# Splitting weights while attention runs: the second halves' word added by VectorE, split sums in the weighted values' bank

## The chip, the cores and the metric

One Trainium2 chip, one core. The metric is the device time of one execution in microseconds. The engines are TensorE (PE for matmuls, PEld for its weight loads), VectorE (DVE), ScalarE (ACT), GpSimd (POOL) and the DMA queues (SPq is issued by SyncE, ACTq by ScalarE). PSUM is what TensorE writes and VectorE and ScalarE read.

## The reference

Attention over 8 batches, 8 heads, 576 positions and 64 channels, where each row keeps its 32 largest scores; the result, as 4608 tokens of 512 channels, goes through a gated feed-forward layer (512 to 1536 to 512). The feed-forward weights are float64, everything else float32.

```python
scores = scale * np.matmul(q, k.transpose(0, 1, 3, 2))
kth = np.partition(scores, -top_k, axis=-1)[..., -top_k:-top_k + 1]
scores = np.where(scores >= kth, scores, -1000000000.0)
attn = np.exp(scores - np.max(scores, axis=-1, keepdims=True))
attn = attn / (np.sum(attn, axis=-1, keepdims=True) + 1e-09)
x = np.matmul(attn, v)        # then to tokens x channels
gate = 1.0 / (1.0 + np.exp(-(x @ w_gate)))
out = (gate * (x @ w_val)) @ w_out
```

## The kernel before

**Attention steps.** `run` (L603) goes through 160 steps: 8 batches, 4 pairs of heads, 5 tiles of rows. In step n TensorE computes the scores of step n + 2 (`begin`, L285 to L328), VectorE and GpSimd choose the 32 largest of step n (`select`), and TensorE transposes the numerators of step n - 2 (`turn`, L425). When a block of tiles is done, `weigh` (L463) multiplies them by the values into one PSUM tile `po` of pool `ps_o`, which has one buffer, and `scale` (L496) lets VectorE divide by the sums (`xf`, L485) and ScalarE and GpSimd split the result into two float32r parts, `xh` and `xl`.

**Feed-forward.** `ffn` (L514) works on 256 tokens at first and on 384 later. Each product is made of three float32r matmuls (L540 to L542 into `pz`, L564 to L566 into `po2`, shown as `po`), with weights in two parts. `pz` and `po2` are in pool `ps_f`, with three buffers. `more` runs as many of these matmuls between the pieces of a step as a table (`PACE`) allows.

**Splitting the weights.** Each of the 18 weight tiles [128, 2, 512] of float64 arrives as pairs of 32-bit words and is split half by half, 36 halves in all. `split_front` (L179) makes `bits`, a float32 from the upper word (ScalarE L190, VectorE L191, L192), `power`, its exponent in bfloat16 (VectorE L193, one buffer), `frac`, the lower word as a number (ScalarE L195) times `power` (GpSimd L197, two pieces), and `pair[:, 0]`, the upper part of the word rounded to float32r (ScalarE L198). `split_back` (L201) forms the rest on TensorE in a PSUM tile `rest` of pool `ps_f`: `ident` times `bits` (L205, a float32 matmul, which the trace shows as two instructions), minus `pair[:, 0]` (L206), plus 2**-52 times `frac` (L207). ScalarE copies `rest` into `pair[:, 1]` (L209), and the ScalarE queue issues the DMA that stores the pair in DRAM for later units (L210). `bits` has three buffers.

**When the halves are split.** The first 8 halves (`2 * LOADED`) go one by one through steps 0 to 7, before any feed-forward work. The other 28 are split while the first unit of 256 tokens goes through the feed-forward layer: at each piece of a step at most one `split_back`, once its front is more than three pieces old, and then the next `split_front`, as long as fewer than three halves wait. `load` inside `ffn` also calls both, where a weight is needed that is not ready.

**What sets the order.** TensorE's instructions run in the order of the program, written by hand (`manual_schedule`). The order of each other engine's instructions is set by a planner that runs the program against a model of time; `urgent()` gives an instruction precedence there. A buffer of a pool is written again only when its last reader is done, so pools make engines wait for each other.

Of the kernel before, what the change touches and what calls it, by code (L numbers as in the profile page):

```python
# [10 lines left out]
F32 = mybir.dt.float32  # L11
# [3 lines left out]
F32R = mybir.dt.float32r  # L15
BF16 = mybir.dt.bfloat16
FP8 = mybir.dt.float8e4
AF = mybir.ActivationFunctionType
ALU = mybir.AluOpType
# [11 lines left out]
def tile_topk_attention_then_gated_ffn(  # L31
# [8 lines left out]
    nc = tc.nc  # L40
    P = 128
    B, H, _, S = k.shape
# [10 lines left out]
    M = NP * P  # L53
# [27 lines left out]
    LOADED = 4  # L81
# [8 lines left out]
    bi = ctx.enter_context(tc.tile_pool(name="bi", bufs=4))  # L90
    b2 = ctx.enter_context(tc.tile_pool(name="b2", bufs=2))
    bk = ctx.enter_context(tc.tile_pool(name="bk", bufs=2 * NP))
    bv = ctx.enter_context(tc.tile_pool(name="bv", bufs=3))
    bs = ctx.enter_context(tc.tile_pool(name="bs", bufs=4))
    bq = ctx.enter_context(tc.tile_pool(name="bq", bufs=3))
    bqr = ctx.enter_context(tc.tile_pool(name="bqr", bufs=4))
    bkr = ctx.enter_context(tc.tile_pool(name="bkr", bufs=2))
# [6 lines left out]
    ps_o = ctx.enter_context(tc.tile_pool(name="ps_o", bufs=1, space=bass.MemoryType.PSUM))  # L104
    ps_f = ctx.enter_context(tc.tile_pool(name="ps_f", bufs=3, space=bass.MemoryType.PSUM))

    ident = const.tile([P, P], F32, tag="ident", name="ident")
# [26 lines left out]
    def behind_scores():  # L134
        return tc.issue_after(evicted[-1].ins) if len(evicted) < 12 else ExitStack()

    def urgent():
        return tc.high_priority() if stated else ExitStack()
# [10 lines left out]
    stored, splits, waiting, fetched, ticks, evicted, due, later, pinned, raw_loads = set(), {}, [], {}, [0], [], [], [], [], []  # L149

    pre = ExitStack()
    pre_pools = {n: pre.enter_context(tc.tile_pool(name=n, bufs=bufs)) for n, bufs in (("signs", 1), ("raw", 3), ("parts", 3), ("power", 1))}
    plus, minus = [pre_pools["signs"].tile([P, P], F32R, tag=t, name=t) for t in ("plus", "minus")]
    nc.scalar.activation(plus, ident, AF.Copy, scale=2.0**-52)
    nc.scalar.activation(minus, ident, AF.Copy, scale=-1.0)

    split_order = order[KEPT:LOADED] + order[:KEPT] + order[LOADED:]
    halves_of_weights = [(t, i) for t in split_order for i in range(2)]
# [9 lines left out]
    def load_raw(idx, i):  # L168
        raws[idx, i] = raw = pre_pools["raw"].tile([P, NP * P, 2], U32, tag="raw", name=f"wraw_{idx}_{i}")
        ins = load(raw.rearrange("p n t -> p (n t)"), w[idx][:, i * NP * P : (i + 1) * NP * P].bitcast(U32))  # L170
        raw_loads.append(ins.ins)

    def split_front(idx, i):

        if i == 0:
            splits[idx] = pools["w"].tile([P, 2, 2, NP, P], F32R, tag="w", name=f"wsplit_{idx}")
        at = halves_of_weights.index((idx, i))
        for ahead in halves_of_weights[at : at + 2]:
            if ahead not in raws:  # L179
                load_raw(*ahead)  # L180
        raw = raws[idx, i]
        low, top = raw[:, :, 0], raw[:, :, 1]
        pair = splits[idx][:, i].rearrange("p a c n -> p a (c n)")
        bits = pre_pools["parts"].tile([P, NP * P], F32, tag="bits", name=f"wbits_{idx}_{i}")
        frac = pair[:, 1]
        word = bits.bitcast(U32)
        power = pre_pools["power"].tile([P, NP * P], BF16, tag="power", name=f"wpower_{idx}_{i}")
        heads = bits.bitcast(U16).rearrange("p (n t) -> p n t", t=2)[:, :, 1]
        with behind_scores():
            nc.scalar.activation(bits, top.bitcast(F32), AF.Copy, scale=2.0**-112)  # L190
        nc.vector.tensor_scalar(word, word, 3, None, op0=ALU.logical_shift_left)  # L191
        nc.vector.scalar_tensor_tensor(word, top, 0x80000000, word, op0=ALU.bitwise_and, op1=ALU.bitwise_or)  # L192
        nc.vector.tensor_scalar(power.bitcast(U16), heads, 0xFF80, None, op0=ALU.bitwise_and)  # L193
        with behind_scores():
            nc.scalar.activation(frac, low, AF.Copy)  # L195
        for c in (slice(0, 2 * P), slice(2 * P, 4 * P)):
            nc.gpsimd.tensor_tensor(frac[:, c], frac[:, c].bitcast(F32), power[:, c], op=ALU.mult)  # L197
        nc.scalar.activation(pair[:, 0], bits, AF.Copy)  # L198
        waiting.append((idx, i, pair, bits, ticks[0]))

    def split_back():  # L201
        idx, i, pair, bits, _ = waiting.pop(0)
        frac = pair[:, 1]
        rest = ps_f.tile([P, M], F32, tag="f", name=f"wrest_{idx}_{i}")
        nc.tensor.matmul(rest, ident, bits, start=True, stop=False)  # L205
        nc.tensor.matmul(rest, minus, pair[:, 0], start=False, stop=False)  # L206
        nc.tensor.matmul(rest, plus, frac, start=False, stop=True)  # L207
        with urgent():
            nc.scalar.activation(pair[:, 1], rest, AF.Copy)  # L209
        nc.scalar.dma_start(w_split[idx][:, i], pair.bitcast(F32))  # L210
        if i == 1:
            stored.add(idx)
# [23 lines left out]
    def next_front():  # L236
        while len(waiting) > 2:
            split_back()
        split_front(*due.pop(0))
# [94 lines left out]
    def masked(J, s, kth, st, e, nm, place=None):  # L334

        for j in range(J):
            nc.vector.scalar_tensor_tensor(  # L337
                e[:, j], s[:, j], kth[j], e[:, j], op0=ALU.is_ge, op1=ALU.mult, accum_out=st[:, 4 + j : 5 + j]
            )
        nc.vector.tensor_scalar(st[:, 4 : 4 + J], st[:, 4 : 4 + J], 1e-9, None, op0=ALU.add)  # L340
        if place is not None:
            x, k, rows = place
            invs = inverses[x]
            sums = st[:, 4:6] if J == 2 else st[:, 4:5].to_broadcast([P, 2])
            nc.vector.reciprocal(invs[:, k:8:4], sums)
            if k == 3:
                turned_invs = b6[0].tile([P, 32], F32, tag="invt", name=f"invt_{nm}")
                nc.vector.transpose(turned_invs, invs)
                for x in range(4):
                    nc.sync.dma_start(rows[:, 32 * x : 32 * x + 32], turned_invs[32 * x : 32 * x + 8])  # L350
            return e, None
        nc.vector.reciprocal(st[:, 6 : 6 + J], st[:, 4 : 4 + J])
        inv = bi.tile([P, P], F32, tag="inv", name=f"inv_{nm}")
        nc.gpsimd.tensor_copy(
            inv.rearrange("p (j d) -> p j d", j=J), st[:, 6 : 6 + J].unsqueeze(2).to_broadcast([P, J, P // J])
        )
        return e, inv
# [19 lines left out]
    def select(J, s, col, nm, place):  # L377
# [42 lines left out]
        for j in range(J):  # L420
            nc.vector.max(kths[:, at[j] : at[j] + 8], u[:, j])  # L421
        yield masked(J, s, [kths[:, a + 7 : a + 8] for a in at], st, e, nm, place)

    def turn(e, inv, i, et, nm):
# [85 lines left out]
    def ffn(nm0, xs, t0, width, early, last):  # L510
# [7 lines left out]
        def load(idx):  # L518
            if not (t0 == 0 and early):
                return stored_weight(idx, nm0)  # L520
            first_weights(order.index(idx))
            while idx not in stored:
                if not waiting:
                    next_front()
                split_back()
            return fetched[idx]
# [72 lines left out]
    def run(general):  # L599
# [160 lines left out]
        for n in range(len(steps) + 3):  # L760
# [6 lines left out]
            if splitting:  # L767
                split_front(*fronts.pop(0))
# [24 lines left out]
            else:  # L793
# [9 lines left out]
                for t, chunk in enumerate(chunks):  # L803
                    ticks[0] += 1
                    if not fronts and not splitting:
                        if waiting and ticks[0] - waiting[0][4] > 3:
                            split_back()
                        if due and len(waiting) < 3:
                            next_front()
                    if chunk is not None:  # L810
                        next(chunk, None)
                        while unfinished and t == 0:
                            weighted(*unfinished.pop(0))
                    elif 3 <= n:
                        weighed(n - 3)
                        if n == OPEN:
                            weighed(n - 2)
                    if t == 2 and splitting and len(waiting) > 1:
                        split_back()
                    if n != OPEN or t > 0:  # L820
                        more(begun + (goal - begun) * (t + 1) / len(chunks))
# [84 lines left out]
```

## Time and profile before

| | |
|---|---|
| median of 3 runs | 1576.34 us (1575.83 to 1578.79) |
| profiled execution, its own time | 1575.44 us |
| its span, first to last instruction | 1573.6 us |
| TensorE busy | 1500.9 us (95%) |
| VectorE busy | 1289.7 us (82%) |
| ScalarE busy | 1151.0 us (73%) |
| GpSimd busy | 1106.5 us (70%) |
| granted TensorE clock, mean | 0.988 of 2.4 GHz |

The page gives the share of busy time of each engine over the whole span. Since the kernel has stages with different limits, the tables by stretch, the waits and the chain have to be read beside it. Ends of matmuls are modelled; what one matmul really takes is read from the distance between the starts of two that follow each other.

### The profile page before, as it was taken

To read this page: it belongs to the slowest core of one execution; us is meant where nothing else is said; L and a number is where in the kernel's file an instruction comes from. 1 tells how busy PE (TensorE), PEld (TensorE's weight loads), DVE (VectorE), ACT (ScalarE), POOL (GpSimd) and SP (SyncE) were. 2 spreads that over 40 slices of the span, in tenths; PEclk is the share of its full clock that TensorE was granted. 3 is DMA by queue.
4 is the path that set the end of the run, shared out by engine and by line. 5 is a ranking of instruction groups with operands and counts; after the bars stand their busy time and mean duration, and the time that the engine had idled before them with its cause. 6 is when DMAs were issued, how large, how long until landed. Compare 5 with 4: busy or idle time off the path is not lost.

```text
span 1573.6 us, 33616 instructions
## 1 busy us (share of the span) xinstructions
PE 1500.9 (95%) x10242; PEld 1310.9 (83%) x10242; DVE 1289.7 (82%) x5996; ACT 1151.0 (73%) x2520; POOL 1106.5 (70%) x1656
## 2 busy tenths in 40 slices
PE   5777999999999999999999999999999999999998
PEld 2355768988898899888898899888898899889897
DVE  7988878899999788999888788999888788998001
ACT  6868987888687678777777778777777778777321
POOL 4657897698776876887775876887775876775312
PEclk9889999999999999999999999999999999999999
DMA  6426878778665676676565675676555666564575
GB/s 204 151 93 221 274 274 303 270 250 299 228 214 190 228 260 204 212 254 211 198 210 190 228 257 206 213 251 213 199 209 190 228 224 224 198 217 168 208 271 186
DMA packets 96240, 347.34 MB, mean 221 GB/s; under 512 B 13105, under 2 KB 33585, under 8 KB 68273
## 3 DMA queue, kind: packets, MB, share of 16 engines
q1 hardware_dynamic: 90864, 326.22, 60.4%
q10 hardware_dynamic: 5184, 18.88, 3.0%
q8 instruction: 83, 1.36, 0.4%
q14 instruction: 109, 0.88, 0.2%
HBM read 316.60 MB, written 28.45 MB: 219 GB/s over the span
## 4 chain that ended last, share of the span: by engine, by line
PE 63%; DVE 11%; POOL 4%; ACT 4%; issue 2%; DMA 2%; ACTq 0%; SPq 0%; DVEq 0%; POOLq 0%
PE pz L540 10%; PE pz L542 9%; PE pz L541 9%; PE pss L316 7%; PE po L480 7%; PE pt L432 5%; PE po L564 5%; PE po L566 5%; PE po L565 5%; DVE e L337 3%; DVE cand L394 3%; POOL u L413 2%; DVE kths L421 2%; DVE cand L400 1%; ACT under L407 1%
## 5 line engine op out<-in xcount | busy, mean ns | idle before, releaser
L413 POOL TENSOR_TENSOR u<-s,under 128x288 f32<-128x288 f32 x576 | 423.9, 760 | 128.8 <-ACT under L407 124.1
L540 PE MATMUL pz<-xh,w 128*128 128x384 f32 (+1 forms) x1152 | 404.3, 351 | 0.0
L394 DVE MAX8 cand<-s 128x8 f32<-128x72 f32 x2304 | 352.9, 217 | 38.1 <-ACT s L324 26.5
L542 PE MATMUL pz<-xh,w 128*128 128x384 f32 (+1 forms) x1152 | 377.4, 328 | 0.0
L541 PE MATMUL pz<-xl,w 128*128 128x384 f32 (+1 forms) x1152 | 376.9, 327 | 0.0
L407 ACT ACTIVATE under<-s,leads 128x576 fp8e4<-128x576 f32 x288 | 222.6, 773 | 103.8 <-DVE leads L398 97.0
L337 DVE SCALAR_TENSOR_TENSOR e<-s,kths,e 128x576 f32<-128x576 f32 x288 | 282.9, 990 | 15.0 <-ACT e L332 14.4
L421 DVE MAX8 kths<-u 128x8 f32<-128x584 f32 x288 | 219.3, 761 | 66.1 <-POOL u L414 63.6
L552 POOL TENSOR_TENSOR gl<-gf,gh 128x384 fp32r<-128x384 f32 (+1 forms) x156 | 156.3, 1002 | 121.1 <-ACT gh L551 118.1
L540 PEld LDWEIGHTS pz<-xh,w 128*128 128x128 f32 x1152 | 217.1, 188 | 5.7 <-DVE tops L398 1.3
L332 ACT ACTIVATE e<-s,st 128x576 f32<-128x576 f32 x288 | 208.9, 771 | 15.7 <-PE pt L432 10.7
L541 PEld LDWEIGHTS pz<-xl,w 128*128 128x128 f32 x1152 | 217.7, 189 | 0.8
L542 PEld LDWEIGHTS pz<-xh,w 128*128 128x128 f32 x1152 | 216.5, 188 | 0.0
L438 ACT ACTIVATE ring<-pt 128x384 f32<-128x384 f32 x336 | 163.5, 496 | 56.9 <-PE pt L432 56.0
L432 PE MATMUL pt<-ident,e 128*128 128x128 f32 x1152 | 191.9, 276 | 7.8 <-ACT ring L438 7.8
L432 PEld LDWEIGHTS pt<-ident,e 128*128 128x128 f32 x1152 | 147.2, 141 | 39.4 <-ACT ring L438 11.2
L564 PE MATMUL po<-w,gh 128*128 128x512 f32 x408 | 173.1, 424 | 1.2 <-DVE gf L550 1.2
L324 ACT ACTIVATE s<-pss 128x576 f32<-128x576 f32 x256 | 164.2, 641 | 8.8 <-PE pss L316 8.3
L316 PE MATMUL pss<-k,qh 128*128 128x288 f32 (+2 forms) x588 | 162.2, 294 | 8.2 <-ACT s L324 7.9
L550 DVE SCALAR_TENSOR_TENSOR gf<-gf,pz 128x384 f32<-128x384 f32 (+1 forms) x156 | 79.7, 511 | 102.6 <-PE pz L542 90.4
L565 PE MATMUL po<-w,gl 128*128 128x512 f32 x408 | 160.9, 394 | 2.8 <-POOL gl L552 2.8
L566 PE MATMUL po<-w,gh 128*128 128x512 f32 x408 | 161.3, 395 | 0.0
(115 smaller groups left out, 3315.8 us busy)
## 6 DMA issues: line engine op xcount, KB each, us to landing
w<-ws SPq DMA_DIRECT2D x216, 1024.0 KB
v<-in_v_dram SPq DMA_DIRECT2D x68, 320.0 KB
wraw<-in_w_dram SPq DMA_DIRECT2D x36, 512.0 KB
ws<-wsplit ACTq DMA_DIRECT2D x36, 512.0 KB
qraw<-in_q_dram SPq DMA_DIRECT2D x140, 128.0 KB
kraw<-in_k_dram SPq DMA_DIRECT2D x56, 288.0 KB
out_dram<-acc SPq DMA_DIRECT2D x36, 256.0 KB
invb<-rows SPq DMA_DIRECT2D x66, 128.0 KB
```

Source lines behind the costliest of these rows:

```text
L316: nc.tensor.matmul(ps[:, half, o : o + n], x[:K, h * P : (h + 1) * P], ks[h][:K, k0 : k0 + n], start=t == 0, stop=t == len(todo) - 1,)
L337: nc.vector.scalar_tensor_tensor(e[:, j], s[:, j], kth[j], e[:, j], op0=ALU.is_ge, op1=ALU.mult, accum_out=st[:, 4 + j : 5 + j])
L394: nc.vector.max(cand[:, j, 8 * g : 8 * g + 8], s[:, j, g * SEG : (g + 1) * SEG])
L413: nc.gpsimd.tensor_tensor(u[:, j, c], s[:, j, c], under[:, j, c], op=ALU.mult)
L421: nc.vector.max(kths[:, at[j] : at[j] + 8], u[:, j])
L432: nc.tensor.transpose(pt[:, c], ef[:, k0 : k0 + P], ident)
L540: nc.tensor.matmul(ps[:, R], wt[:, u, 0, d], xh[:, R], start=d == 0, stop=False)
L541: nc.tensor.matmul(ps[:, R], wt[:, u, 0, d], xl[:, R], start=False, stop=False)
L542: nc.tensor.matmul(ps[:, R], wt[:, u, 1, d], xh[:, R], start=False, stop=d == NP - 1)
L564: nc.tensor.matmul(outs[r], gh, wh, start=f == 0, stop=False)
L565: nc.tensor.matmul(outs[r], gl, wh, start=False, stop=False)
L566: nc.tensor.matmul(outs[r], gh, wl, start=False, stop=f == FG - 1)
```

## The change

- In `split_back`, second halves (`i == 1`) that are not among the first 8 get no `ident` times `bits` matmul. The accumulation begins with minus `pair[:, 0]`, and VectorE adds `bits` when it reads `rest`, in place of ScalarE's copy. All other halves keep matmul and copy.
- `rest` is taken from pool `ps_o` (one buffer, shared with `po` of the weighted values), no longer from `ps_f`.
- `frac` is scaled by -2**-52 when ScalarE makes it, so that `minus` serves for both matmuls; `plus` and the instruction that makes it are gone.
- `power` has two buffers. `inv` moves from a pool with four buffers to one of its own with three.

```diff
+    binv = ctx.enter_context(tc.tile_pool(name="binv", bufs=3))
...
-    pre_pools = {n: ... for n, bufs in (("signs", 1), ("raw", 3), ("parts", 3), ("power", 1))}
-    plus, minus = [pre_pools["signs"].tile([P, P], F32R, tag=t, name=t) for t in ("plus", "minus")]
-    nc.scalar.activation(plus, ident, AF.Copy, scale=2.0**-52)
+    pre_pools = {n: ... for n, bufs in (("signs", 1), ("raw", 3), ("parts", 3), ("power", 2))}
+    minus = pre_pools["signs"].tile([P, P], F32R, tag="minus", name="minus")
     nc.scalar.activation(minus, ident, AF.Copy, scale=-1.0)
...
-            nc.scalar.activation(frac, low, AF.Copy)
+            nc.scalar.activation(frac, low, AF.Copy, scale=-(2.0**-52))
...
-        rest = ps_f.tile([P, M], F32, tag="f", name=f"wrest_{idx}_{i}")
-        nc.tensor.matmul(rest, ident, bits, start=True, stop=False)
-        nc.tensor.matmul(rest, minus, pair[:, 0], start=False, stop=False)
-        nc.tensor.matmul(rest, plus, frac, start=False, stop=True)
+        rest = ps_o.tile([P, M], F32, tag="o", name=f"wrest_{idx}_{i}")
+        added = i == 1 and (idx, i) not in halves_of_weights[: 2 * LOADED]
+        if not added:
+            nc.tensor.matmul(rest, ident, bits, start=True, stop=False)
+        nc.tensor.matmul(rest, minus, pair[:, 0], start=added, stop=False)
+        nc.tensor.matmul(rest, minus, frac, start=False, stop=True)
         with urgent():
-            nc.scalar.activation(pair[:, 1], rest, AF.Copy)
+            if added:
+                nc.vector.tensor_tensor(pair[:, 1], rest, bits, op=ALU.add)
+            else:
+                nc.scalar.activation(pair[:, 1], rest, AF.Copy)
         nc.scalar.dma_start(w_split[idx][:, i], pair.bitcast(F32))
...
-        inv = bi.tile([P, P], F32, tag="inv", name=f"inv_{nm}")
+        inv = binv.tile([P, P], F32, tag="inv", name=f"inv_{nm}")
```

## Rows read from the trace of the kernel before

**Rows 1.** The page: busy time by engine, and the chain that ended last.

```profile
PE 1500.9 (95%) x10242; PEld 1310.9 (83%) x10242; DVE 1289.7 (82%) x5996; ACT 1151.0 (73%) x2520; POOL 1106.5 (70%) x1656
...
PE 63%; DVE 11%; POOL 4%; ACT 4%; issue 2%; DMA 2%; ACTq 0%; SPq 0%; DVEq 0%; POOLq 0%
```

**Rows 2.** Windows: stretch, length, busy us by engine, clock, DMA share, GB/s.

```profile
118.00:157.00 39.00, 31.05 (x164) 20.18 (x162) 34.47 (x128) 33.58 (x70) 30.76 (x45) 1.00 0.66 223
157.00:197.00 40.00, 38.41 (x219) 28.45 (x217) 35.84 (x117) 36.22 (x75) 32.60 (x43) 1.00 0.81 272
197.00:245.00 48.00, 44.07 (x234) 30.92 (x233) 36.70 (x112) 40.63 (x84) 43.98 (x63) 1.00 0.81 274
...
245.00:1560.00 1315.00, 1301.35 (x9229) 1180.97 (x9226) 1077.93 (x5141) 956.04 (x2125) 932.52 (x1390) 1.00 0.65 225
```

**Rows 3.** The chain that ended last, 196 to 245 us, shares by line.

```profile
by line: DMA kraw<-in_k_dram 24.4%; ACT wsplit L195 7.0%; issue 6.8%; ACT wbits L190 4.7%; DVE wbits L192 4.4%; ACT k L265 3.9%; POOL k L267 3.6%; DVE e L337 3.4%; ACT wsplit L198 3.4%; DVE wbits L191 3.3%; PE po L480 3.3%; ACT wsplit L209 
```

**Rows 4.** One tile, wrest, 118 to 245 us: duration ns min/median/max, starts, forms.

```profile
L205 PE MATMUL wrest<-wbits,ident x56: 590/592/697, 120.1 to 241.1; 128*128 128x512 f32 x56
...
L209 ACT ACTIVATE wsplit<-wrest x28: 572/592/653, 125.7 to 243.5; 128x512 fp32r<-128x512 f32 x28
```

**Rows 5.** Timeline of TensorE: start us, us, instruction; one half of the 28.

```profile
229.14 1.02 PE L205 MATMUL wrest<-wbits,ident 128*128 128x512 f32 x2
229.60 0.79 PE L206 MATMUL wrest<-wsplit,minus 128*128 128x512 f32 x1
230.23 0.39 PE L207 MATMUL wrest<-wsplit,plus 128*128 128x512 f32 x1
230.46 0.29 PE L316 MATMUL pss<-k,qh 128*128 128x288 f32 x1
```

**Rows 6.** TensorE's waits, 118 to 245 us: us in total, times, longest.

```profile
PE wrest L205 <- DVE gf L550: 6.4, 5, 2.4
PE pz L540 <- ACT wsplit L209: 3.7, 3, 2.1
...
PE wrest L205 <- ACT wsplit L209: 1.4, 2, 1.0
```

**Rows 7.** Timeline, TensorE and ScalarE: longest and shortest wait for the copy.

```profile
130.16 0.39 PE L207 MATMUL wrest<-wsplit,plus 128*128 128x512 f32 x1
...
136.72 0.57 ACT L209 ACTIVATE wsplit<-wrest 128x512 fp32r<-128x512 f32 x1
...
188.47 0.40 PE L207 MATMUL wrest<-wsplit,plus 128*128 128x512 f32 x1
...
189.02 0.59 ACT L209 ACTIVATE wsplit<-wrest 128x512 fp32r<-128x512 f32 x1
...
189.75 1.04 PE L205 MATMUL wrest<-wbits,ident 128*128 128x512 f32 x2
```

**Rows 8.** Timeline around 210 us: weighted values right behind a first half.

```profile
210.04 0.43 PE L480 MATMUL po<-ring,v 128*64 128x256 f32 x1
...
213.77 0.60 ACT L209 ACTIVATE wsplit<-wrest 128x512 fp32r<-128x512 f32 x1
```

**Rows 9.** VectorE by line and form, whole span: busy us, mean ns, idle before.

```profile
L550 DVE SCALAR_TENSOR_TENSOR gf<-gf,pz 128x384 f32<-128x384 f32 x120 | 65.1, 543 | 96.6 <-PE pz L542 87.0 <-ACT gf L547 9.2
...
L575 DVE SCALAR_TENSOR_TENSOR acc<-po,acc 128x512 f32<-128x512 f32 x3 | 2.1, 692 | 6.2 <-PE po L566 5.5 <-DMA out_dram<-acc 0.7
```

**Rows 10.** Waits of VectorE, then of ScalarE, 118 to 245 us.

```profile
DVE wpower L193 <- POOL wsplit L197: 8.2, 9, 2.4
DVE wbits L191 <- ACT wbits L190: 5.7, 3, 2.5
...
ACT wsplit L198 <- DVE wbits L192: 5.3, 4, 2.4
```

**Rows 11.** Windows, a later stretch of 20 us.

```profile
340.00:360.00 20.00, 19.14 (x137) 18.19 (x138) 19.23 (x101) 16.70 (x38) 17.68 (x26) 0.91 0.85 267
```

**Rows 12.** Timeline of TensorE: the stand at 340 us.

```profile
340.86 0.56 PE L565 MATMUL po<-w,gl 128*128 128x512 f32 x1 [2.78 <-POOL gl L552]
```

More of the change, by code (lines that the diff above doesn't have):

```diff
@@ L151, in tile_topk_attention_then_gated_ffn @@
     pre = ExitStack()
-    pre_pools = {n: pre.enter_context(tc.tile_pool(name=n, bufs=bufs)) for n, bufs in (("signs", 1), ("raw", 3), ("parts", 3), ("power", 1))}
-    plus, minus = [pre_pools["signs"].tile([P, P], F32R, tag=t, name=t) for t in ("plus", "minus")]
-    nc.scalar.activation(plus, ident, AF.Copy, scale=2.0**-52)
+    pre_pools = {n: pre.enter_context(tc.tile_pool(name=n, bufs=bufs)) for n, bufs in (("signs", 1), ("raw", 3), ("parts", 3), ("power", 2))}
+    minus = pre_pools["signs"].tile([P, P], F32R, tag="minus", name="minus")
     nc.scalar.activation(minus, ident, AF.Copy, scale=-1.0)
```

## The prediction

> **What bounds the kernel now.** The page comes first: TensorE is busy for 95% of the span, the next engine, VectorE, for 82%, and 63% of the chain that ended last lies on TensorE [rows 1]. So the kernel as a whole is bound by TensorE, and whatever is won before a stretch in which TensorE never stands is won at the end. The windows say where that holds [rows 2]. From 245 us on, when the last weight is split, TensorE is busy for 1301 of 1315 us. From 118 to 245 us, where the 28 halves are split that the change touches, four engines are nearly full: summed over the three windows of 127 us, TensorE 113.5, ScalarE 110.4, VectorE 107.0, GpSimd 107.3 us. Then I read the chain for the end of this stage [rows 3]: between 196 and 245 us it runs over key loads (24.4%) and over splitting and attention work of ScalarE, VectorE and GpSimd; TensorE appears there only with `po` (3.3%), behind the last half. So in the splitting stage TensorE's work is not simply the bound, and TensorE, whose order is fixed, often stands for a buffer.
>
> **TensorE's work.** Of the 28 halves (L209 28 times, L205 56 times, two for each [rows 4]), 14 are second halves. What L205 really takes is read from starts [rows 5]: a half lasts 230.46 - 229.14 = 1.32 us; L207 takes 230.46 - 230.23 = 0.23, and L206 has the same shape and type, so 1.32 - 2 x 0.23 = 0.86 us are L205's. 14 x 0.86 = 12.0 us of TensorE's work go.
>
> **TensorE's stands for `ps_f`.** L205 waited 6.4 us for VectorE's `gf` and 1.4 us for ScalarE's L209; both are waits for one of three `ps_f` buffers, and go, since `rest` no longer lies there. `pz` waited 3.7 us for L209 [rows 6]. The smallest of the three, 0.4 us, is `pz` waiting for its own weights, and stays; 3.3 go. Together 6.4 + 1.4 + 3.3 = 11.1 us.
>
> **New stands for `ps_o`.** There is one buffer now for `rest` and `po`, so the matmuls of a half wait until the half before has been read, and `po` waits for the half before it. TensorE runs in order: behind such a wait stand feed-forward, transposes and scores. The trace of before has no such wait, so I bound it. From the end of L207 to the end of L209 a first half took between 0.74 us (189.61 - 188.87) and 6.74 us (137.29 - 130.55) [rows 7], in the mean of the 14 first halves 3.0 us; the following second half came about 1.0 us after L207's end (0.88 in rows 7), stands taken off. If all copies came as fast as the fastest one, 13 pairs would cost nothing; if all stay as late as they were, the differences pair by pair add up to 25.0 us. At four places `po` or its reader stands right beside a half. The clearest is at 210.04 us, where `po` begins while the copy of the first half in front of it ends at 214.37 [rows 8]. With the shortest latencies these places cost 2.9 us in all, with the recorded ones 12.2. So the new stands lie between 2.9 and 37.2 us. I take a latency of 1.8 us, midway between fastest and mean: ScalarE loses 14 copies of 0.592 us, 8.3 of its 110.4 busy us [rows 2, 4], and works off its queue whenever TensorE stands. 13 x (1.8 - 1.0) = 10.4, and 6 for the four places: 16.4 us.
>
> TensorE's balance: 12.0 + 11.1 - 16.4 = 6.7 us won.
>
> **VectorE.** It gets 14 additions of 128x512 from PSUM and SBUF into float32r. The nearest row is the last accumulation, L575, same shape and one operand in PSUM: 692 ns; 128x384 took 543 ns [rows 9], which is the low end. 14 x 0.692 = 9.7 us. The second buffer of `power` ends its waits of 8.2 us for GpSimd [rows 10]: L193 no longer stands for the half before. What is late next is L191 for ScalarE (5.7 us), which has less to do than before. VectorE's position changes by 9.7 - 8.2 = +1.5 us (between -8.2 and +9.7 if only one holds). It has 20 us without work in these 127, and I count 1.5 us against the gain.
>
> **ScalarE.** The copies save 8.3 us. Against that its queue now holds 14 DMA issues (L210 of before) that wait for VectorE's addition instead of ScalarE's own copy, and behind each stand its next activations. The nearest row is ScalarE's wait for VectorE at L198: 5.3 us over 26 instructions, 4 of them waiting [rows 10], 0.2 us each, so 14 x 0.2 = 2.8 us; bounds 0 and 14 x 2.4 = 34 us, the longest wait every time. ScalarE stays ahead by about 5.5 us, which covers this. [...]
>
> **Costed at nothing.** The scale in L195 is a field of an instruction that runs anyway. `plus` was made in the opening, before there is anything to split. `bits` of a second half is held until the addition, up to some 2 us longer; a front of three halves later needs it, and halves come 4.5 us apart (127 / 28). `inv` with three buffers: written in one step and read in the next, so two are alive. The first 8 halves now share `ps_o` with `po` too, but before the feed-forward work begins, when TensorE has least to do; if that cover is gone, four meetings at the shortest latency cost 3 us. The planner will order the later stages anew: it may lose or repeat a stand like the 2.78 us at 340.86 [rows 12], a few us of either sign, and I take 0.
>
> **Sum.** -6.7 + 1.5 = -5.2 us. The profiled execution took 1575.4 us, 0.9 less than the median; 1575.4 - 5.2 = 1570.2, and on the median's footing 1571.
>
> **Rivals.**
> 1. *The three others decide, no change.* For it: TensorE's 3.3% of the chain in [rows 3], and VectorE at 107 + 9.7 = 117 of 127 us. Against it: TensorE is 96% busy from 157 to 197 us [rows 2]. Then only VectorE's +1.5 us and a part of ScalarE's gain count: between -2 and +5 us, 1574 to 1581, in the middle 1577.
> 2. *The one bank stops TensorE, slower.* Place: each second half behind its first half, and `po` behind a half. For it: the mean latency was 3.0 us, and the gain is used up from 2.3 us on ((12.0 + 11.1 - 6) / 13 + 1.0 = 2.3). Against it: ScalarE was late partly because it stood itself for VectorE [rows 10], whose longest cause goes. Price with latencies as recorded: 25.0 + 12.2 - 23.1 = +14 us, 1590; most likely half of it, 1583. A long stand can also lower the clock: behind the stand of 2.78 us [rows 12] the mean granted clock of 20 us was 0.91 [rows 11], so a part ran at 1.2 GHz, which costs 0.09 x 20 = 1.8 us each time, while the 2.4 us stand of [rows 6] left 1.00 [rows 2]. [...]
> 3. *The copies follow at once, much faster.* For it: latencies of 0.74 us occur. 12.0 + 11.1 - 2.9 = 20 us at most; ScalarE and VectorE, at 84 to 87% of the stage, will not let all of it through: -10 to -18 us, in the middle 1562.
> 4. *It does not do what it says:* excluded, the matmuls are left out in the program, and TensorE's order is the program's.
>
> **From cases to numbers.** My forecast (-2 to -10 us, 1566 to 1574) has 0.45, of which 0.07 lie within 0.2% (3.2 us, what a measurement here can tell from no change). Rival 1 has 0.20 (0.14 within, 0.06 slower), rival 2 has 0.18, rival 3 has 0.17. Faster 0.38 + 0.17 = 0.55, same 0.21, slower 0.24. The range reaches from -15 to +6 us and leaves out about 0.05 of rival 3 and 0.11 of rival 2: 1561 to 1582.
>
> **What will show it.** 28 matmul instructions of L205 fewer, all in second halves; the 14 additions near 0.69 us; no wait of L193 for L197; no wait of TensorE's `rest` for `gf`. TensorE's waits for L209, the addition and `xf` at `rest` and `po` should sum to about 16 us; above 23 the forecast is wrong in that term. The stage that ended at 245 us should end about 5 us earlier, and the rest of the span should shift with it; if the stage ends earlier but the end does not, a later stage took it back.

## Result: slower, and where the time went

The changed kernel takes 1589.0 us (1588.9 to 1589.5, 4 runs) against 1576.4 before; the ratio is 1.0082 (95% interval 1.0068 to 1.0095). 1571 was forecast, with 1561 to 1582 as the range: the wrong side, and outside. The page of the changed kernel, engines and chain, answers to [rows 1]:

```profile
PE 1497.7 (94%) x10214; PEld 1312.5 (83%) x10214; DVE 1295.8 (82%) x6010; ACT 1144.9 (72%) x2505; POOL 1100.5 (69%) x1656
...
PE 66%; DVE 11%; ACT 6%; POOL 4%; issue 2%; DMA 2%; SPq 0%; ACTq 0%; DVEq 0%; POOLq 0%
```

28 TensorE instructions are gone, but its busy time fell by 3 us, not by 12. To see why, I compare the stage over the same work in every kernel: from the 73rd feed-forward matmul to the 180th transpose. Windows of the kernel before, and of the changed kernel (columns as in [rows 2]):

```profile
119.40:255.10 135.70, 122.22 (x681) 87.03 (x681) 112.53 (x370) 116.02 (x239) 113.76 (x159) 1.00 0.77 262
```

```profile
122.50:268.80 146.30, 118.99 (x654) 88.77 (x653) 118.99 (x382) 110.20 (x225) 108.99 (x159) 0.92 0.73 243
```

The stage begins 3.1 us late and lasts 10.6 us longer; it ends 13.7 us late. The span is 14.1 us longer, so the 1319 us behind the stage cost nothing worth naming. The 10.6 us have three parts. TensorE stood for 135.7 - 122.2 = 13.5 us before and for 146.3 - 119.0 = 27.3 after: +13.8. The granted clock was 1.00 and is 0.92: by my estimate up to 0.08 x 146.3 = 11.7 us of the busy time are there only because a part of it ran at half clock. Windows of 1 us of the changed kernel give 0.50 from 220 to 222 us, and matmuls of 512 columns start 0.43 us apart there (219.75, 220.18, 220.60, 221.03); at 1.00 they start 0.23 us apart (254.83, 255.06, 255.28, 255.51). The 1.2 and 2.4 GHz of the recorded texts are these clocks of 0.50 and 1.00: 512 columns in 0.427 us are 1.2 per ns, which by estimate makes 2.4 at 1.00, where 0.23 us show 2.2. What is left, the work at full clock, is 119.0 - 11.7 = 107.3 instead of 122.2: -14.9. 13.8 + 11.7 - 14.9 = 10.6. (The clock is given to 0.01, so the last two are good to 0.7 us, and TensorE also stood in a little of the time at half clock, 1.7 of the 3 us from 185 to 188, so both are rather too large than too small.) Work was saved as forecast, a little more even; stands and the lower clock took it back and more.

TensorE's waits in the changed kernel from 118 to 262 us, which answer to [rows 6], with L207 the identity matmul, L208 and L209 the two with `minus`, L214 ScalarE's copy, L212 VectorE's addition:

```profile
PE wrest L208 <- ACT wsplit L214: 21.6, 9, 3.8
PE po L485 <- DVE wsplit L212: 2.0, 2, 1.0
PE wrest L208 <- DVE xf L490: 1.6, 1, 1.6
PE wrest L207 <- DVE xf L490: 1.1, 1, 1.1
PE po L485 <- ACT wsplit L214: 0.9, 1, 0.9
```

Each of the five is a wait for the one buffer of `ps_o`, and they sum to 27.2 us. The waits for `ps_f` of [rows 6] are gone. The longest, in the timeline of ScalarE and TensorE:

```profile
217.23 0.57 ACT L214 ACTIVATE wsplit<-wrest 128x512 fp32r<-128x512 f32 x1
...
217.86 0.50 PE L208 MATMUL wrest<-wsplit,minus 128*128 128x512 f32 x1 [3.80 <-ACT wsplit L214]
218.19 0.39 PE L209 MATMUL wrest<-wsplit,minus 128*128 128x512 f32 x1
```

The second half's first matmul starts 0.06 us after the copy of its first half ends, and no other TensorE work comes in between: windows of 1 us from 215 to 217 us show it busy for 0.00 us. Nine of 14 second halves stand like this.

VectorE and ScalarE in the changed kernel: the addition, the DMA issue's wait in ScalarE's queue (duration ns min/median/max), and two of VectorE's waits, which answer to [rows 10]:

```profile
L212 DVE TENSOR_TENSOR wsplit<-wrest,wbits x14: 667/676/692, 133.0 to 256.4; 128x512 fp32r<-128x512 f32 x14
...
L215 ACTq EVENT_SEMAPHORE  x16: 17/17/2304, 125.7 to 255.1; - x16
```

```profile
DVE wbits L191 <- ACT wbits L190: 10.7, 10, 2.3
...
DVE wpower L193 <- POOL wsplit L197: 0.5, 1, 0.5
```

### The profile page after: what moved, and what is told of

Its sections match the earlier page's. It is cut to its first block, busy times and chain, and to the rows that moved or that the text cites. A ratio compares the mean times of both kernels' runs of the same rounds, so it can differ in the third digit from the quotient of the medians.

```text
span 1587.7 us, 33557 instructions
## 1 busy us (share of the span) xinstructions
PE 1497.7 (94%) x10214; PEld 1312.5 (83%) x10214; DVE 1295.8 (82%) x6010; ACT 1144.9 (72%) x2505; POOL 1100.5 (69%) x1656
## 4 chain that ended last, share of the span: by engine, by line
PE 66%; DVE 11%; ACT 6%; POOL 4%; issue 2%; DMA 2%; SPq 0%; ACTq 0%; DVEq 0%; POOLq 0%
PE pz L545 10%; PE pz L547 9%; PE pz L546 9%; PE pss L321 8%; PE po L485 7%; PE pt L437 6%; PE po L569 5%; PE po L570 5%; PE po L571 5%; DVE cand L399 3%; DVE e L342 3%; DVE kths L426 2%; POOL u L418 2%; DMA kraw<-in_k_dram 1%; ACT under L412 1%
## 5 line engine op out<-in xcount | busy, mean ns | idle before, releaser
L412 ACT ACTIVATE under<-s,leads 128x576 fp8e4<-128x576 f32 x288 | 222.6, 773 | 107.3 <-DVE leads L403 97.7
L557 POOL TENSOR_TENSOR gl<-gf,gh 128x384 fp32r<-128x384 f32 (+1 forms) x156 | 156.7, 1005 | 124.7 <-ACT gh L556 121.7
L337 ACT ACTIVATE e<-s,st 128x576 f32<-128x576 f32 x288 | 208.9, 770 | 19.3 <-PE pt L437 13.8
```

## The experiments

Four edits make the change's parts; the first kernels put them back or do them alone.

**The bank put back.** `rest` lies in `ps_f` again.

```diff
-        rest = ps_o.tile([P, M], F32, tag="o", name=f"wrest_{idx}_{i}")
+        rest = ps_f.tile([P, M], F32, tag="f", name=f"wrest_{idx}_{i}")
```

> The changed kernel with the split sums back in the three-buffer pool of the feed-forward layer; the addition on VectorE, the folded scale and the second exponent buffer stay. Theory 1 (the one shared bank costs the time, by TensorE standing behind the copy of each first half and by the lower clock behind such stands): 1566 to 1573 us, no stand of TensorE at minus-times-word for the copy, clock 1.00 from 118 to 240 us. Theory 2 (the work moved to VectorE costs the time: 14 additions of 0.68 us, and DMA issues of ScalarE that wait for them): 1582 to 1590 us, as the changed kernel. Theory 3 (a new order by the planner, no one part): near 1580.

1575.4 us, ratio to before 1.0003 (0.9993 to 1.0012): the whole loss is gone, and no gain shows. So the shared bank cost 13 us, but the forecast of what is left without it was wrong too, and none of the three expected times came. The same stretch and TensorE's waits, 100 to 250 us:

```profile
120.80:254.70 133.90, 117.51 (x655) 86.29 (x654) 118.07 (x394) 109.44 (x224) 108.87 (x155) 0.95 0.79 268
```

```profile
PE wrest L209 <- POOL wsplit L197: 6.8, 7, 3.0
...
PE wrest L207 <- DVE wsplit L212: 2.9, 2, 2.3
PE wrest L208 <- ACT wsplit L198: 2.6, 1, 2.6
```

TensorE stands 6.8 us at L209 for GpSimd's product of the lower word, where the kernel before stood 1.8 us (118 to 245 us), and the clock is 0.95 (0.05 x 133.9 = 6.7 us).

**The bank alone**, on the kernel before (the same line, the other way).

> The kernel before with one edit: the split sums lie in the one-buffer pool of the weighted values. Theory 1: slower than before by 10 to 25 us, 1586 to 1601, since the stands come without the 12 us of matmuls saved. Theory 2: within 3 us of before, 1573 to 1579. Theory 3: 1576 to 1585.

1594.7 us, ratio 1.0117 (1.0097 to 1.0138), as the first theory has it. One line costs 18 us where no matmul is saved. Its stretch, and TensorE's waits from 118 to 270 us (L209 is the copy here, L205 the identity matmul):

```profile
123.60:276.90 153.30, 127.46 (x682) 90.56 (x681) 114.47 (x370) 117.71 (x240) 109.97 (x159) 0.96 0.70 233
```

```profile
PE wrest L205 <- ACT wsplit L209: 16.9, 9, 4.1
PE po L480 <- ACT wsplit L209: 5.8, 3, 3.0
PE wrest L205 <- DVE xf L485: 3.2, 2, 2.2
```

The stands are those of the changed kernel, without VectorE's addition: they belong to the bank.

**The addition alone**, on the kernel before (three `ps_f` buffers, one exponent buffer).

```diff
+        added = i == 1 and (idx, i) not in halves_of_weights[: 2 * LOADED]
+        if not added:
+            nc.tensor.matmul(rest, ident, bits, start=True, stop=False)
-        nc.tensor.matmul(rest, ident, bits, start=True, stop=False)
...
+            if added:
+                nc.vector.tensor_tensor(pair[:, 1], rest, bits, op=ALU.add)
+            else:
+                nc.scalar.activation(pair[:, 1], rest, AF.Copy)
-            nc.scalar.activation(pair[:, 1], rest, AF.Copy)
```

> The kernel before with one edit: 14 second halves get no identity matmul and VectorE adds the word as it reads the sum; three-buffer pool, one exponent buffer. Theory 1: faster than before by 3 to 9 us, 1567 to 1573, as 12 us of TensorE work go and no new bank is shared. Theory 2: slower by 5 to 14 us, 1581 to 1590. Theory 3: 1573 to 1582.

1578.1 us, ratio 1.0019 (1.0010 to 1.0029): 12 us of matmuls less, and slower by 3 us. Only the third theory's range held it. Its stretch shows 24.1 us of stands (139.1 - 115.0) and a clock of 0.96:

```profile
120.70:259.80 139.10, 115.02 (x654) 84.51 (x653) 121.70 (x384) 109.38 (x226) 113.22 (x159) 0.96 0.75 257
```

**The small parts alone**, measured twice, ten executions each: the changed kernel with `ps_f` and `added = False`.

> The kernel before with the small parts of the change alone: scale folded into the lower word, two exponent buffers, three buffers for the inverse sums; no addition on VectorE, split sums in the three-buffer pool. Theory 1 and 2: VectorE's waits of 8.2 us for GpSimd at the exponent go, of which a part arrives: 1571 to 1576 us. Theory 3: any of 1571 to 1582.

> The small parts of the change alone, once more with more rounds (1572.7 us against 1575.1 before, 0.14%): two exponent buffers, scale folded in, three buffers for the inverse sums. If the gain is real: 1571 to 1574 us and an interval wholly under 1. If it was chance: 1574 to 1577.

1572.7 us, ratio 0.9986 (0.9976 to 0.9995), and 1573.1, ratio 0.9981 (0.9971 to 0.9990): 2 to 3 us faster than before, the fastest of all kernels here. In the stretch TensorE has all its work and the full clock:

```profile
120.90:252.30 131.40, 122.47 (x682) 87.08 (x681) 113.00 (x379) 114.77 (x239) 109.36 (x155) 1.00 0.81 273
```

**The bank for the later halves only.** The first 8 halves use `ps_f`, the other 28 `ps_o`.

```diff
+        late_half = (idx, i) not in halves_of_weights[: 2 * LOADED]
+        rest = (ps_o if late_half else ps_f).tile([P, M], F32, tag="o" if late_half else "f", name=f"wrest_{idx}_{i}")
-        rest = ps_o.tile([P, M], F32, tag="o", name=f"wrest_{idx}_{i}")
```

> The changed kernel, but the first 8 halves have their split sums in the three-buffer pool; the 28 later ones stay in the one shared bank. The opening was 3.1 us behind at the start of the splitting stage in the changed kernel and the stage added 10.6. If the shared bank costs in both stages independently: 1584 to 1587 us. If the stage's loss alone decides: 1587 to 1590. If the late opening was what set the stage off: 1575 to 1580.

1582.8 us, ratio 1.0046 (1.0030 to 1.0063), between the expected ranges and in none of them. Some 6 us of the loss come back. Its stretch shows where:

```profile
121.30:263.10 141.80, 119.33 (x654) 88.86 (x653) 116.88 (x394) 110.10 (x225) 106.05 (x155) 0.93 0.75 254
```

The stage begins 1.2 us earlier than in the changed kernel (121.3 against 122.5) and is 4.5 us shorter (141.8 against 146.3), though the 28 halves in it use the same bank. So only 1.2 us of the changed kernel's 3.1 us of delay go with the bank in the opening. Inside the stage TensorE stands 22.5 us instead of 27.3. A new order of the other engines' instructions may be why, but no run shows it.

**More distance between halves**, same bank.

```diff
-                        if waiting and ticks[0] - waiting[0][4] > 3:
+                        if waiting and ticks[0] - waiting[0][4] > 3 and ticks[0] - backed[-1] > 1:
```

(`backed` notes the piece in which the last half's matmuls were issued.)

> The changed kernel with one condition more: a half's matmuls come at the earliest two pieces after those of the half before, so that more of TensorE's other work stands between a first half and its second. Work, bank and readers stay. If the loss is the wait of a second half's matmuls for the copy of its first half (2.45 us from matmul end to copy end in the mean, at some 1 us distance): most of the 21.6 us of stands goes, 1576 to 1582 us. If the loss is the sharing as such, of sums with weighted values: 1586 to 1591.

1579.1 us, ratio 1.0023 (1.0014 to 1.0033), in the first range: 9 us of the loss come back. TensorE's waits from 118 to 262 us and the stretch (L210 is the first `minus` matmul here, L216 the copy):

```profile
PE wrest L210 <- ACT wsplit L216: 7.1, 4, 2.7
PE po L573 <- DVE wsplit L214: 5.8, 4, 1.7
```

```profile
122.40:260.00 137.60, 113.65 (x655) 84.00 (x654) 119.06 (x383) 109.15 (x225) 111.47 (x159) 0.98 0.75 256
```

Second halves stand 7.1 us for the copy instead of 21.6, though the copy comes as late as ever: from the last matmul of a first half to the end of its copy 2.37 us in the mean of 14, against 2.45 in the changed kernel. For this wait what counted was how much other work TensorE had in between. But other stands came in its place: all stands of the stretch sum to 24.0 us, only 3.3 less than in the changed kernel. The larger part of the gain is the clock, 0.98 instead of 0.92, up to 11.7 - 2.8 = 8.9 us.

**Two buffers of the transposes' pool** in place of `ps_o` (`rest = ps_t.tile(...)`, tag "t").

> The changed kernel with the split sums in the two-buffer pool of the transposes instead of the one-buffer pool. If one buffer is what costs: two let a second half begin before its first half is read, 1575 to 1581 us. If any bank whose other tenant ScalarE must copy costs as much: 1586 to 1592.

1584.0 us, ratio 1.0044 (1.0030 to 1.0058), between the two ranges. Its first feed-forward matmul starts at 111.5 us, 11.9 later than before, and the stage begins at 127.3 us, 7.9 later, and ends at 267.6, 12.5 later: in the profiled execution most of its loss comes from the opening, where transposes are dense. It does not tell one buffer from a shared one.

**The word left out**: `ps_f`, no identity matmul for the 14 halves, and ScalarE copies.

```diff
-            if added:
-                nc.vector.tensor_tensor(pair[:, 1], rest, bits, op=ALU.add)
-            else:
-                nc.scalar.activation(pair[:, 1], rest, AF.Copy)
+            nc.scalar.activation(pair[:, 1], rest, AF.Copy)
```

> Split sums in the three-buffer pool, two exponent buffers; 14 second halves get no identity matmul and ScalarE copies the sum as it is, so the word is not added anywhere (left out to measure). TensorE's 12 us are saved and VectorE has no addition. If TensorE's matmuls were on the path and VectorE's additions ate the gain: 1562 to 1569 us. If TensorE's work in this stage was never on the path: 1571 to 1574, as with the small parts alone.

1576.9 us, ratio 1.0007 (0.9997 to 1.0016), above both ranges. Against the small parts alone nothing was added anywhere, 14 matmuls were taken out, and by the two ratios it is 3 to 4 us slower. So VectorE's additions are not what ate the gain. The stretch:

```profile
121.70:261.00 139.30, 122.78 (x654) 92.20 (x653) 112.94 (x378) 114.76 (x237) 109.48 (x155) 0.89 0.76 257
```

A clock of 0.89 over 139.3 us costs 15.3 us by the same estimate, more than the 12.0 us that were saved, and the stands grew from 8.9 us (131.4 - 122.5) to 16.5. This profile is of the slowest of the ten executions (1580.5 us). Over all ten the mean clock of the whole execution was 0.981 to 0.987, in the middle 0.985, against 0.990 with the small parts: by my estimate 0.005 x 1577 = 8 us. So in a usual execution the clock takes back a large part of the 12.0 us, and the stands the rest.

**The matmuls back, their product thrown away.** As bank_back, but the 14 identity matmuls run and the next matmul starts the sum anew; in a second kernel they cover half the columns.

```diff
-        if not added:
-            nc.tensor.matmul(rest, ident, bits, start=True, stop=False)
+        nc.tensor.matmul(rest, ident, bits, start=True, stop=added)
```

> Split sums in the three-buffer pool, VectorE adds the word, and the 14 identity matmuls run again, but their product is thrown away (the next matmul starts the sum anew): TensorE has its 12 us back, all else is as in bank_back, which took 1575.4 us with 6.8 us lost to the lower clock in the stage. Theory of the clock (the saved matmuls are paid back because TensorE, with less to do, falls to 1.2 GHz): no time at 1.2 GHz between 120 and 240 us, and the time within 3 us of bank_back, 1573 to 1578, although 12 us of work were added. Theory of a full price (the matmuls are on the path, and VectorE's additions were the loss): 1583 to 1588.

> As filled, but the identity matmul that is thrown away covers 256 of 512 columns, 6 us of work in all. Theory of the clock: if half the work holds the clock at 2.4 GHz, faster than filled and bank_back, 1567 to 1572; if not, 1574 to 1579 with some us at 1.2 GHz. Theory that ScalarE, VectorE and GpSimd decide the stage and TensorE's work does not count: the same as bank_back and filled, 1574 to 1577.

1575.5 us, ratio 0.9993 (0.9984 to 1.0002), and with half the columns 1579.4, ratio 1.0017 (1.0008 to 1.0027). The stretch of the first, then of the second:

```profile
120.60:255.30 134.70, 123.69 (x682) 88.38 (x681) 121.13 (x394) 109.31 (x224) 110.74 (x155) 0.99 0.79 267
```

```profile
120.50:257.90 137.40, 122.73 (x683) 92.08 (x682) 119.76 (x393) 108.94 (x223) 110.25 (x155) 0.95 0.77 261
```

12 us of useless work change nothing. By the windows the work of bank_back at full clock was 117.5 - 6.7 = 110.8 us and that of filled is 123.7 - 1.3 = 122.4; against the 11.6 us more stand 16.4 - 11.0 = 5.4 us fewer stands and 6.7 - 1.3 = 5.4 us less lost to the clock. Not only the profiled executions say so: the mean clock of the whole execution was 0.988 to 0.992 in the eleven of filled and 0.983 to 0.988 in the ten of bank_back. With half the columns there is half the work and a clock as low as without any (0.984 to 0.987), so it is slower than both, and a little above the highest range expected. Had TensorE's work simply not counted, it would have taken the same time as they did. The expectation for filled was no time at all at half clock; 0.99 says that a little was left, and the time is the one expected.

## Why the prediction was wrong, point by point

At the end of the stage, where 5.2 us less were forecast, the profiled execution is 13.7 us late, a miss of 18.9. It is made up of the clock (nothing forecast, up to 11.7 measured), TensorE's stands (16.4 - 11.1 = 5.3 more forecast, 13.8 measured, a miss of 8.5), the opening (nothing forecast, 3.1 measured) and, the other way, 2.9 us more of TensorE's work saved than forecast and the 1.5 us set aside for VectorE: 11.7 + 8.5 + 3.1 - 2.9 - 1.5 = 18.9.

- **"14 x 0.86 = 12.0 us of TensorE's work go" and are won.** The work went; the time did not come. This is the first step that failed, and it failed without the shared bank too. filled takes the time of bank_back, and no_word is slower than the small parts alone: in this stage the matmuls filled time in which TensorE would otherwise stand for GpSimd, ScalarE or VectorE, and with fewer of them more of the rest ran at half clock (a mean of 0.95 in bank_back's stretch, 0.99 in that of filled). I had the warning in hand, a chain with 3.3% of TensorE [rows 3], and made it a rival instead of a factor on the term. (The row ends early; in the whole chain TensorE has 2.2 of 49 us, all of it at the end.)
- **"Stands for `ps_f` ... 11.1 us go."** They went, as the waits show. With three buffers and fewer matmuls others came in their place (6.8 us for L197).
- **"I take a latency of 1.8 us ... 16.4 us" for `ps_o`.** Right mechanism, wrong size, and the second step that failed: 27.2 us in the stage, with a mean latency of 2.45 us. ScalarE did not work off its queue as fast as I argued: its copies came 0.55 us earlier than before (3.0), not 1.2. The 27.2 us are above the 23 at which the forecast counted as wrong in this term, and nearer to its upper bound, 37.2, than to the lower.
- **The clock.** I priced it in rival 2 only, 1.8 us for each stand as long as [rows 12]. It cost up to 11.7 us in the changed kernel, in a stage that had run at 1.00 before. The sum had no term for it, and this is the largest single miss.
- **VectorE: +1.5 us.** Its parts were right: 14 additions of 0.68 us (0.69 forecast), the wait at L193 down from 8.2 to 0.5 us. What was late next was L191 for ScalarE, as named, but it grew from 5.7 to 10.7 us.
- **ScalarE: 14 waits at DMA issues, 2.8 us.** At the DMA issues ScalarE's queue shows 16 waits of 17 ns in the median and 2.3 us at most, 5.1 us in all, of which three make up 4.9. A part of that passed while an activation was still running, so the 2.8 us were of the right size. The bound of 34 us, the longest wait every time, was far off: few of the waits were long. In the longest, from 131.44 to the issue at 133.78 us, one activation starts at 131.97, as the one before it ends; the next starts at 134.16, behind the issue. The scale in L195, costed at nothing, cost nothing: L195 takes 0.67 us in the median with it, 0.68 without.
- **The opening, "costed at nothing", 3 us if the cover is gone.** The stage begins 3.1 us late, and TensorE has waits for the bank before 118 us that have no counterpart before:

```profile
PE po L485 <- ACT wsplit L214: 2.0, 2, 1.0
PE wrest L207 <- DVE xf L490: 1.2, 1, 1.2
```

But the seven edited kernels whose first 8 halves use `ps_f` begin the stage 1.1 to 2.3 us late as well (120.5 to 121.7 us against 119.4), bank_later 1.9. So the cover was gone in part only: against bank_later the bank is worth 1.2 us of the 3.1; alone, in bank_alone, which begins the stage at 123.6, it came with 4.2. Where the rest of the 3.1 comes from is open.

- **The later stages, taken as 0:** right. The stand of 2.78 us [rows 12] is there again, 14 us later and 2.80 us long.

Rival 2 named the place and, with latencies as recorded, the time (1590). That the time agrees is in part luck, for it got there with another sum: 37 us of stands less 23 gained, where the runs show about 14 more us of stands in the stage, up to 12 of clock, 3 in the opening, and 15 of work saved.

What stays open: how much of the saved work would have arrived at a clock of 1.00. Every kernel without those matmuls has both more stands and a lower clock, and no run separates the two. The planner also orders each kernel anew, so single differences of 2 to 4 us between these kernels may hold some of that.

## What to carry to other kernels

Work taken from the engine that is 90% busy is won only if nothing else is late at the same place (here 12.0 us of work less brought nothing); look at what each of its next waits is for before counting it. A buffer moved to a pool of one made the next writer wait for the last reader's queue here, 27.2 us in all in the stage, so price it with the latencies as recorded, not with those that would be nice. And in a stage in which TensorE often stands, saved matmuls can be paid back in its clock, as in no_word, 0.89 against 1.00 with the small parts: put a term for it into the sum, and look at the clock of all executions, not only of the profiled one.

## What the runs showed of the hardware

The lower clock came behind shorter stands than I had priced. In no_word TensorE counted as busy for 122.8 of 139.3 us and the mean granted clock was 0.89; the kernel before, busy for 122.2 of 135.7, held 1.00. One place of no_word: windows of 10 us, and TensorE's waits from 200 to 212 us:

```profile
190.00:200.00 10.00, 10.00 (x56) 7.98 (x56) 8.55 (x23) 8.98 (x19) 9.84 (x14) 1.00 0.82 285
200.00:210.00 10.00, 6.55 (x19) 4.12 (x18) 8.30 (x18) 6.11 (x12) 8.98 (x12) 0.77 0.74 218
210.00:220.00 10.00, 10.00 (x34) 7.05 (x33) 6.62 (x24) 8.76 (x18) 8.74 (x12) 0.72 0.93 326
220.00:230.00 10.00, 10.00 (x69) 7.74 (x67) 7.96 (x13) 9.04 (x18) 9.84 (x13) 1.00 0.89 321
```

```profile
PE wrest L208 <- DVE gf L552: 1.9, 1, 1.9
PE po L566 <- ACT wsplit L211: 1.6, 1, 1.6
```

Two stands of 1.9 and 1.6 us, close together, and the clock is 0.77 in the mean of this window and 0.72 in the next, in which TensorE does not stand at all: there matmuls of 512 columns start 0.43 us apart from 211.92 to 213.20 us, where they were 0.23 to 0.24 apart just before the two stands (199.75 to 200.22), and TensorE counts as busy for 10 of 10 us and gets 34 matmuls done where the window after it has 69 (their kinds differ). A full row of busy time is no proof of a full clock. Nor does the length of a single stand tell: the kernel before stood 2.4 us once in this stage [rows 6] and kept 1.00.
